# Routing without index transfers, six experts in whole float32 passes, SiLU taken from ScalarE's table

## The chip, the core and the metric

One core of one Trainium2 chip runs the whole program in one launch. The metric is device time in microseconds (us). The engines are PE (TensorE: matrix products; PEld is its weight load), DVE (VectorE), ACT (ScalarE), POOL (GpSimd) and SP (SyncE, which here only issues transfers). Each engine takes its own instructions strictly in the order in which they were written, and waits on semaphores for the others.

## What is computed

The reference, cut to what matters:

```python
# attention, 2 batches x 8 heads, 768 positions, 64 wide: a pair counts only if 6 sign bits of q@proj, k@proj agree
scores = where(q_bucket == k_bucket, q @ k.T / 8, -1e9)
x = (softmax(scores) @ v).reshape(1536, 512)          # 1536 tokens
# mixture of 8 experts, 192 tokens each, assigned greedily by descending logit
for idx in argsort(-(x @ w_gate).flatten()):
    tok, e = divmod(idx, 8)
    if assigned[tok] >= 0 or counts[e] >= 192: continue
    assigned[tok] = e; counts[e] += 1
for e in range(8): out[assigned == e] = relu(x[assigned == e] @ w1[e]) @ w2[e]   # 512 -> 1024 -> 512
# second layer on all tokens
h = out @ w_in; g = h / (1 + exp(-h)); result = g @ w_out                        # 512 -> 2048 -> 512
```

Everything is float32; `w_in` and `w_out` arrive as 64-bit floats and are turned into float32 on the chip.

## The kernel before, in words

**Attention** fills the first 280 us, and writes the tokens to a DRAM array `xd`. The change leaves its code alone.

**Routing** goes in eight phases (`route(ph)`). A phase fills one expert. It finds the logit at which some expert reaches 192 tokens by a search of seven counting steps (`count`): DVE compares all tokens with 63 to 78 thresholds (`cmp`, L577), PE sums the comparisons (L581, into `rp`), DVE turns the sums into a mask (`ok`, L584), PE picks the threshold (L587), DVE reads it (L588) and forms the next thresholds. So DVE and PE take turns, and the next phase needs the phase before. At the end stands the count of tokens per expert (`cnt`, L694). The next phase's head (L609 to L621: `pen`, `Lm`, `M`, `eq`, `mr`, `cthr`, `Bw`) needs only that count.

**Slots** (`slots(ph)`) turn a phase into a list of 192 tokens: the expert's number `ei` (L703 to L709, read by SP into a register, by which it loads that expert's weights), ranks (L713 to L719, a PE product `rpp` at L725, L729, L730), twelve one-hot matrices `oh` (L734), a product with the token numbers on PE (`rpi`, L740) and the integer list `TI` (L743). POOL then gathers the tokens from `xd` in two indirect transfers of 96 rows (L750, into `xg`), and PE transposes them (`px`, L757).

**An expert** (`expert(ph)`) is 8 blocks of a first product and 4 of a second. For the experts of phases 0 to FP-1 the product is in whole float32 (`whole`, L813; 4 matmuls of 192 columns are one planner's part). For the others the weights are split in a rounded half and a rest (`whi` on ACT, L781; `wlo` on POOL or DVE, L783), and the product is 4 matmuls of 384 columns (L800) and 4 of 192 (L801), whose halves ACT and DVE add (`t`, L789, L790), and split again (`H`, L842, `xhl`, L764).

**The second layer** (`second(gi)`) takes two experts' 384 tokens at once, in split form: A is 16 blocks of three products (L884); a block's sum `mm` goes through ACT (sigmoid, `sg`, L890), DVE (times `mm`, L891), ACT (rounded copy `gh`, L894) and DVE (rest `gl`, L895); B (L910) sums blocks into `acc`, which is scattered to the output by an indirect transfer (L919). The token list for that scatter is written by SP to a DRAM array `idxd` (L745) and read back as `ix` (L872). The weights of A and B are converted from 64-bit words once (`Weights.plan`): a load of half a megabyte into `craw` (L461), and passes on ACT (L465, for some halves L471) and DVE (L467, L468, L469, L470 or POOL L472), 28 halves in this part of the program.

**The order** on each engine comes from a planner (`Plan.run`, L38): every operation has a duration, a key and dependencies, and is taken by earliest start and then by key. Routing phases below `RU` have key -1e6, which lets nothing delay them by more than a tolerance; later ones come `RO` before their expert. `GA` is the planned transfer time of a gather, `dma` that of a weight load. These numbers steer only the order in which instructions are written; on the chip an instruction waits for its data, and all behind it on its engine wait too.

Of the kernel before, what the change touches and what calls it, by code (L numbers as in the profile page):

```python
# [9 lines left out]
F32 = mybir.dt.float32  # L10
# [414 lines left out]

FP = 4

NW = 4; NH = 3; NG = 4; NCW = 2

GROUPS = ((0, 1), (2, 3), (4, 5), (6, 7)); SKEW = (6, 0, 0, 0); RU = 2; RO = 250; CK = 200  # L430

GA = 3.4

# [7 lines left out]
class Weights:  # L441
# [10 lines left out]
    def plan(self, P, a, b, key, pool, ring, after=lambda m: []):  # L452

        nc=self.nc; V=nc.vector; raw={}
        for m in range(a,b):
# [17 lines left out]
            k=key+m  # L473
            P.op(("c64",m),"SP",.45,load,after(m),k,ring,dma=1.46)
            P.op(("cv",m,0),"Activation",.53,c0,[("c64",m)]+([("cv",m-1,0)] if h else []),k)
# [44 lines left out]

def moe(ctx, tc, L, xd, idxd, w1, w2, MW, K, ident, out):
    nc=tc.nc; V=nc.vector; G=nc.gpsimd; A_=nc.scalar
# [17 lines left out]
    Lc=c1.tile([128,12,8],F32,name="Lc")  # L540
    TI=c1.tile([96,16],I32,name="TI")
    def b12(x): return x[:,:,None].to_broadcast([128,12,8])
# [56 lines left out]
    def route(ph):  # L599
# [97 lines left out]
    def slots(ph):  # L697

        ch=Chain(("S",ph),[T_["end",ph]])
        def s0():  # L700
# [44 lines left out]
        def wr_(): nc.sync.dma_start(idxd[ph*192:(ph+1)*192,:].rearrange("(c p) o -> p (c o)",p=96),TI[:,2*ph:2*ph+2])  # L745
        op(("ix",ph),"SP",.2,wr_,[t],rk(ph),after=2.2)
        for c in range(2):
            def ga(c=c):
                xg=T_["xg",ph,c]=fx.tile([96,512],F32,name="xg",tag="xg")
                G.indirect_dma_start(out=xg,out_offset=None,in_=xd,in_offset=bass.IndirectOffsetOnAxis(ap=TI[:,2*ph+c:2*ph+c+1],axis=0))  # L750
            op(("g",ph,c),"Pool",1.25,ga,[t]+([("xt",ph-1,1)] if ph else []),rk(ph)+c*.01,dma=GA,slack=1.5)
# [115 lines left out]
    def second(gi):  # L867
        g=GROUPS[gi]; nt=3
        ydeps=[("Y",ph,db,1) for ph in g for db in range(4)]
        def ix():  # L870
            T_["IX",gi]=fx.tile([128,3],I32,name="ix",tag="ix")
            nc.sync.dma_start(T_["IX",gi],idxd[g[0]*192:g[0]*192+384,:].rearrange("(c p) o -> p (c o)",p=128))  # L872
        op(("IX",gi),"SP",.2,ix,[("ix",ph) for ph in g]+([("sc",gi-2,t) for t in range(3)] if gi>1 else []),0,after=2.2)
        for c in range(8):
            u=("A",gi,c); key=KEY[u]
            weights(u,2*c,([("cv",m,3) for m in (4*c,4*c+1) if m>=NC] if gi==0 else [("hi",("A",0,c))])+([("hi",("B",gi,c-2))] if c>1 else [("hi",("w2",g[-1],3))]+([("hi",("B",gi-1,7))] if gi else [])),key)
            for o in range(2):
# [14 lines left out]
                def gh(nm=nm):  # L892
# [40 lines left out]
def kernel(ctx: ExitStack, tc: tile.TileContext, q, k, v, proj, w_gate, w1, w2, w_in, w_out, out):  # L933
# [41 lines left out]
```

## Time and profile before

| | |
|---|---|
| median of 3 runs | 878.95 us (875.61 to 879.46) |
| profiled execution | 879.95 us, of which span 878.2 us |
| PE | 765.3 us busy, 87% of the span |
| DVE | 645.7 us busy, 74% |
| ACT | 446.5 us busy, 51% |
| POOL | 409.8 us busy, 47% |
| mean granted clock of TensorE | 0.916 |

Busy shares are averages over stages: attention to about 280 us, routing phase 0 alone to about 330 us, experts, routing and second layer mixed to about 704 us, and then PE without a pause to 870 us. What a change is worth is read from the stage in which it lies. The granted clock is 1.00 where the chip lets TensorE run at 2.4 GHz and 0.50 at 1.2 GHz.

### The profile page before, as it was taken

The page shows a single profiled execution, that of the slowest core. Times are in us where ns is not written, and L with a number is a line of the kernel's source. Part 1 is how long each engine was busy: PE and PEld are TensorE (multiplying, and loading weights), DVE is VectorE, ACT ScalarE, POOL GpSimd, SP SyncE. Part 2 cuts the span into 40 slices and gives each one's busy share as a digit, 9 for nine tenths or more (in the row PEclk, how much of TensorE's full clock was granted, in tenths as well). Part 3 has the DMA queues.
Part 4 walks back from the last instruction along what each step waited for, and adds up shares of the span by engine and source line. Part 5 has one row for each costly group of instructions (what it writes and reads, how often), then busy time and mean ns, then how long its engine had stood idle before and what let it go on. Part 6 is the DMA issues. An engine that isn't in the chain of part 4 may idle for free.

```text
span 878.2 us, 16341 instructions
## 1 busy us (share of the span) xinstructions
PE 765.3 (87%) x6117; PEld 675.4 (77%) x6117; DVE 645.7 (74%) x1541; ACT 446.5 (51%) x845; POOL 409.8 (47%) x295
## 2 busy tenths in 40 slices
PE   4988998999995349888998999897978999999996
PEld 3777887887784239776787888786868999999895
DVE  6788988869875887687899546798889576765441
ACT  2587887888884102153353232443443565655442
POOL 4276678778884000043443212244345554555442
PEclk9699999999997558896999799898998999999999
DMA  8958474763301265854364425401513732200000
GB/s 198 223 162 207 110 179 112 162 154 87 95 19 66 96 150 157 211 168 144 66 192 145 43 80 140 100 25 10 150 51 19 172 93 78 76 21 29 8 1 36
DMA packets 106559, 93.03 MB, mean 106 GB/s; under 512 B 33032, under 2 KB 92424, under 8 KB 106480
## 3 DMA queue, kind: packets, MB, share of 16 engines
q1 hardware_dynamic: 104496, 85.70, 36.8%
q0 software_dynamic: 1984, 6.29, 4.7%
q8 instruction: 48, 0.79, 0.4%
q14 instruction: 31, 0.25, 0.1%
HBM read 66.09 MB, written 6.30 MB: 82 GB/s over the span
## 4 chain that ended last, share of the span: by engine, by line
PE 55%; DVE 27%; issue 7%; DMA 5%; ACT 3%; POOL 2%; SPq 1%; POOLq 0%; DVEq 0%; ACTq 0%
PE mm L884 14%; PE acc L910 11%; PE mm L813 5%; PE mm L800 4%; PE S L300 3%; PE mm L801 3%; PE ST L340 2%; PE ST L341 2%; DMA xg<-xd,TI 2%; DVE wlo L783 2%; DVE cmp L577 2%; PE pm L232 2%; DVE S L302 2%; PE rp L581 2%; DVE m L304 2%
## 5 line engine op out<-in xcount | busy, mean ns | idle before, releaser
L350 POOL TENSOR_TENSOR AH<-Aa,AH 128x768 f16<-128x768 f32 x94 | 159.4, 1712 | 75.1 <-ACT AH L348 61.2
L783 POOL TENSOR_TENSOR wlo<-w,whi 128x512 fp32r<-128x512 f32 x68 | 106.0, 1563 | 138.3 <-ACT whi L781 115.2
L884 PE MATMUL mm<-Y,whi 128*128 128x384 f32 x512 | 113.2, 364 | 3.6 <-DVE ki L633 2.3
L884 PEld LDWEIGHTS mm<-Y,whi 128*128 128x128 f32 x512 | 94.7, 202 | 14.4 <-DVE sg L891 3.8
L345 ACT ACTIVATE Aa<-ST 128x384 f32<-128x384 f32 x192 | 87.8, 496 | 27.9 <-PE ST L341 26.9
L783 POOL TENSOR_TENSOR wlo<-wraw,whi 128x512 fp32r<-128x512 f32 x35 | 57.2, 1641 | 72.4 <-ACT whi L781 62.7
L300 PE MATMUL S<-k,q 76*128 76x384 f32 x192 | 74.1, 406 | 12.7 <-DVE m L304 5.8
L348 ACT CAST AH<-Aa 128x768 f16<-128x768 f32 x96 | 80.0, 835 | 0.8
L910 PE MATMUL acc<-whi,gh 128*128 128x512 f32 x192 | 79.9, 416 | 0.0
L581 PEld LDWEIGHTS <-cmp 128*63 128x63 bf16 (+2 forms) x588 | 33.1, 128 | 60.4 <-DVE cmp L577 45.2
L910 PE MATMUL acc<-wlo,gh 128*128 128x512 f32 x192 | 76.5, 398 | 0.0
L910 PE MATMUL acc<-whi,gl 128*128 128x512 f32 x192 | 76.3, 398 | 0.0
L781 ACT CAST whi<-w 128x1024 fp32r<-128x1024 f32 x64 | 67.0, 1047 | 16.9 <-PE acc L910 12.8
L340 PE MATMUL ST<-q,k 128*128 128x384 f32 x192 | 71.5, 372 | 1.4 <-ACT Aa L345 1.4
L783 DVE TENSOR_TENSOR wlo<-w,whi 128x512 fp32r<-128x512 f32 x60 | 53.3, 888 | 25.5 <-ACT whi L781 18.6
L341 PE MATMUL ST<-q,k 97*128 97x384 f32 x192 | 67.2, 350 | 0.7 <-ACT q L325 0.6
L581 PE MATMUL rp<-Bw,cmp 128*63 128x8 bf16 (+2 forms) x588 | 39.1, 185 | 32.2 <-DVE cmp L577 31.7
L364 PE MATMUL av<-vh,AH 128*128 128x66 f16 x576 | 63.6, 195 | 2.0 <-DVE AH L350 1.2
L362 PE MATMUL av<-vh,AH 128*128 128x66 f16 x576 | 64.5, 198 | 0.0
L302 DVE TENSOR_REDUCE S<-S 128x1 f32<-128x385 f32 x96 | 53.6, 559 | 14.6 <-PE S L300 13.7
L363 PE MATMUL av<-vl,AH 128*128 128x64 f16 x576 | 63.6, 194 | 0.0
L894 ACT CAST gh<-sg 128x384 fp32r<-128x384 f32 x64 | 32.7, 513 | 57.1 <-DVE sg L891 57.1
(253 smaller groups left out, 1955.5 us busy)
## 6 DMA issues: line engine op xcount, KB each, us to landing
wraw<-in_moe_w_dram SPq DMA_DIRECT2D x64, 512.0 KB
craw<-in_moe_w_in_dram SPq DMA_DIRECT2D x14, 512.0 KB
craw<-in_moe_w_out_dram SPq DMA_DIRECT2D x14, 512.0 KB
q<-qh SPq DMA_DIRECT2D x31, 192.0 KB
k<-kh SPq DMA_DIRECT2D x15, 384.0 KB
kn<-in_k_dram SPq DMA_DIRECT2D x16, 192.0 KB
qn<-in_q_dram SPq DMA_DIRECT2D x16, 192.0 KB
vn<-in_v_dram SPq DMA_DIRECT2D x8, 384.0 KB
```

Source lines behind the costliest of these rows:

```text
L300: nc.tensor.matmul(SX[y][:,:384],qq[:76,0,s],kk_[:76,0,s2],start=True,stop=True)
L302: if y==0: V.tensor_reduce(SX[0][:,mc0+c:mc0+c+1],SX[0][:,:385],axis=AX.X,op=ALU.max); return
L340: nc.tensor.matmul(ps[:,:384],kk_[:,1,s],qq[:,1,s2],start=True,stop=False)
L341: nc.tensor.matmul(ps[:,:384],kk_[:97,0,s],qq[:97,0,s2],start=False,stop=True)
L345: A_.activation(T_["A",g][:,m],T_["ST",u][:,:384],AF.Exp,scale=0.125)
L348: if e=="Activation": A_.copy(o[:,:,0],T_["A",g])
L350: def lo(e,g=g): (G if e=="Pool" else V).tensor_sub(T_["AH",g][:,:,1],T_["A",g],T_["AH",g][:,:,0])
L581: for b in range(6*h,6*h+6): nc.tensor.matmul(T_[k][:n,:8],cmp[h][:,b-6*h,:],T_["Bw",ph][:,b,:],start=b==0,stop=b==11)
L781: A_.copy(T_["w",u][0],get())
L783: s=slice(h*512,h*512+512); (G if e=="Pool" else V).tensor_sub(T_["w",u][1][:,s],get()[:,s],T_["w",u][0][:,s].bitcast(F32))
L884: nc.tensor.matmul(T_["ps",nm][:,:384],W(d,int(k==2)),T_["Y",gi][int(k==1)][:,d,:],start=k+d==0,stop=k==2 and d==3)
L910: nc.tensor.matmul(T_["acc",gi,t],a[:,s],x[:,o,:],start=c+o==0 and n==0,stop=c==7 and o==1 and n==2)
```

## The change

- The list of tokens goes no more through DRAM. `TI` becomes one tile of 128 x 4 for each group of two experts, laid out as the scatter wants it. The even expert of a group has its slots in rows of 128 and 64, the odd one of 64 and 128, and the odd one's first 64 are computed a second time at the partitions where the scatter reads them; so it has 36 products in place of 24, and three copies. Gathers are of 128 and 64 rows instead of 96 and 96.
- `FP` goes from 4 to 6: experts 4 and 5 use whole float32 passes.
- The second layer's activation is `Silu`, computed twice by ACT from `mm`: once as float32 and once rounded. DVE's multiplication is gone; the copy from `sg` becomes the second `Silu`.
- `RU` 2 to 4, `GA` 3.4 to 2.0, a conversion load's planned time 1.46 to 2.3, a head's 2.2 to 2.7, and some smaller ones. The slots of phase 0 come before everything, and the planner starts the conversion loads after the first gather.

```diff
-FP = 4
+FP = 6
-GROUPS = ((0, 1), (2, 3), (4, 5), (6, 7)); SKEW = (6, 0, 0, 0); RU = 2; RO = 250; CK = 200
-GA = 3.4
+GROUPS = ((0, 1), (2, 3), (4, 5), (6, 7)); SKEW = (6, 0, 0, 0); RU = 4; RO = 250; CK = 200
+GA = 2.0
-            op(nm,eng,dur,fn,self.last+list(deps),rk(self.name[1])+self.n*.001,ring,frees,after)
+            op(nm,eng,dur,fn,self.last+list(deps),rk(self.name[1])+self.n*.001-(1000 if self.name==("S",0) else 0),ring,frees,after)
+        gi,o_=divmod(ph,2); ti_=TI[gi]
+        parts=((3,0,64,0),(2,0,128,64)) if o_ else ((0,0,128,0),(1,0,64,128))
+        also=((1,64,128,0),) if o_ else ()
-            for c in range(2):
+            for c,r0,r1,f in parts+also:
                 for b in range(12):
-                    nc.tensor.matmul(p[:96,c:c+1],T_["oh",ph][:,b,c*96:(c+1)*96],tokid[:,b:b+1],start=b==0,stop=b==11)
+                    nc.tensor.matmul(p[r0:r1,c:c+1],T_["oh",ph][:,b,f:f+r1-r0],tokid[:,b:b+1],start=b==0,stop=b==11)
-        op(("ix",ph),"SP",.2,wr_,[t],rk(ph),after=2.2)
...
-                    T_["sg",nm]=fx.tile([128,384],F32,name="sg",tag="sg"); A_.activation(T_["sg",nm],src(),AF.Sigmoid)
-                def mu(nm=nm,src=src): s=T_["sg",nm]; V.tensor_tensor(s,s,src(),op=ALU.mult)
+                    T_["sg",nm]=fx.tile([128,384],F32,name="sg",tag="sg"); A_.activation(T_["sg",nm],src(),AF.Silu)
-                    A_.copy(T_["g",nm][0],T_["sg",nm])
+                    A_.activation(T_["g",nm][0],src(),AF.Silu)
...
-    MW.plan(P,NC,32,CK,cw,"craw")
+    MW.plan(P,NC,32,CK,cw,"craw",lambda m: [("g",0,1)])
```

**What it moves.** DVE, in routing phase 0, from the second counting step on. The rows `w` are a weight conversion. Before:

```order
L577 TENSOR_TENSOR cmp<-M,th 128x378 x2
L644 TENSOR_TENSOR shP<-sh_187,P 128x63
L467 TENSOR_SCALAR w_4939<-w_4939 128x512
L468 TENSOR_SCALAR w_4939<-w_4939 128x512
L584 TENSOR_TENSOR ok<-rp,cthr 63x8
L467 TENSOR_SCALAR w_4939<-w_4939 128x512
L468 TENSOR_SCALAR w_4939<-w_4939 128x512
L469 SCALAR_TENSOR_TENSOR w_4939<-craw,w_4939 128x512
L588 TENSOR_REDUCE C<-rp_4988 128x1
```

Now:

```order
L578 TENSOR_TENSOR cmp<-M,th 128x378 x2
L645 TENSOR_TENSOR shP<-sh_186,P 128x63
L585 TENSOR_TENSOR ok<-rp,cthr 63x8
L589 TENSOR_REDUCE C<-rp_4978 128x1
L652 TENSOR_TENSOR th<-shP,C 128x63
L654 TENSOR_TENSOR P<-P,C 128x1
```

No conversion stands in phase 0 any more; the first follows in phase 1, in its fourth counting step. In the same way SP issues no `craw` load before the first expert's four weight loads.

PE, around the end of routing phase 1 (`rpc`, the count) in the middle of expert 0. `mm<-xhl,wraw` is its first product, `mm<-H,wraw` its second. Before:

```order
L813 MATMUL mm<-xhl,wraw 128x192 x4
L690 LDWEIGHTS ones
L690 MATMUL rpc<-As,ones 128x8
L813 MATMUL mm<-xhl,wraw 128x192 x8
L725 LDWEIGHTS before
L725 MATMUL rpp<-tot,before 128x1
L813 MATMUL mm<-xhl,wraw 128x192 x4
L813 MATMUL mm<-H,wraw 128x192 x8
```

Now:

```order
L816 MATMUL mm<-H,wraw 128x192 x4
L691 LDWEIGHTS ones
L691 MATMUL rpc<-As,ones 128x8
L816 MATMUL mm<-H,wraw 128x192 x12
L726 LDWEIGHTS before
L726 MATMUL rpp<-tot,before 128x1
```

Before, 20 of expert 0's 64 matmuls stand ahead of that count; now 52 do. The first transposes (`px`) stood behind five of phase 1's counting steps; now they stand behind two.

DVE, from the expert's number of phase 1 on. `fm` opens the ranks of the slots, `pen` the head of phase 2. Before:

```order
L709 CAST ei<-ef 128x1
L713 TENSOR_TENSOR fm<-A_4903,newc 128x96
L715 TENSOR_REDUCE f<-fm 128x12
L717 SCALAR_TENSOR_TENSOR g_5578<-ones,f 128x12
L719 CAST tot<-g_5578 128x1
```

Now:

```order
L710 CAST ei<-ef 128x1
L610 TENSOR_SCALAR pen<-cnt 128x8
L612 TENSOR_TENSOR Lm<-Lc,pen 128x96
L613 TENSOR_REDUCE M<-Lm 128x12
L614 TENSOR_TENSOR eq<-Lm,M 128x96
```

The ten rows of the next phase's head now stand ahead of the ranks of phase 1, as they did in phase 0 before; for phase 0 itself they have moved behind the token list.

## Rows read from the trace of the kernel before

**Rows 1.** Busy time in five stages: us, PE, PEld, DVE, ACT, POOL, clock, DMA.

```profile
331.70:358.60 26.90, 26.17 (x183) 24.38 (x182) 19.81 (x73) 5.29 (x14) 3.57 (x2) 0.94 0.62 128
358.60:365.30 6.70, 3.90 (x41) 2.93 (x41) 5.73 (x22) 1.77 (x4) 0.00 (x0) 0.75 0.99 328
365.30:395.80 30.50, 26.43 (x175) 24.40 (x174) 23.26 (x48) 14.45 (x28) 9.92 (x7) 0.94 0.61 192
395.80:704.00 308.20, 283.44 (x1788) 247.42 (x1788) 237.24 (x624) 121.33 (x227) 115.60 (x85) 0.92 0.40 96
704.00:870.20 166.20, 165.75 (x896) 151.72 (x893) 96.67 (x154) 89.26 (x159) 81.35 (x49) 1.00 0.13 39
```

**Rows 2.** Timeline of PE, its long waits: start, us, ..., [idle before <-releaser].

```profile
406.81 0.16 PE L725 MATMUL rpp<-tot,before 128*128 128x1 bf16 x1 [2.77 <-DVE tot L719]
...
483.63 1.65 PE L884 MATMUL mm<-Y,whi 128*128 128x384 f32 x4 [2.34 <-DVE ki L633]
...
600.10 0.48 PE L581 MATMUL rp<-Bw,cmp 128*63 128x8 bf16 x6 [4.49 <-DVE cmp L577]
...
645.03 0.17 PE L587 MATMUL rp<-ok,ones 77*128 77x8 bf16 x1 [1.44 <-DVE ok L584]
```

**Rows 3.** Timeline of DVE in routing phase 0 and the start of phase 1.

```profile
292.46 1.02 DVE L577 TENSOR_TENSOR cmp<-M,th 128x378 bf16<-128x378 f32 x2
...
294.93 1.02 DVE L577 TENSOR_TENSOR cmp<-M,th 128x378 bf16<-128x378 f32 x2
...
300.78 1.20 DVE L577 TENSOR_TENSOR cmp<-k,thA 128x468 bf16<-128x468 f32 x2
...
309.12 0.16 DVE L609 TENSOR_SCALAR pen<-cnt 128x8 f32<-128x8 f32 x1
...
311.31 0.25 DVE L713 TENSOR_TENSOR fm<-A,newc 128x96 f32<-128x96 f32 x1
```

**Rows 4.** Timeline of POOL: the first gather.

```profile
318.73 1.15 POOL L750 DMA_INDIRECT xg<-xd,TI  x1 [45.38 <-DMA wraw<-in_moe_w_dram]
```

**Rows 5.** Timeline of PE: transposes of expert 0, first matmuls of experts 0 and 1.

```profile
329.55 1.38 PE L757 MATMUL px<-ident,xg 96*128 96x96 f32 x7 [1.60 <-DMA xg<-xd,TI]
...
331.67 2.91 PE L813 MATMUL mm<-xhl,wraw 128*128 128x192 f32 x8
...
365.29 2.93 PE L813 MATMUL mm<-xhl,wraw 128*128 128x192 f32 x8
```

**Rows 6.** Chain that ended last: expert 1's gather; parts of PE at full clock.

```profile
349.86 2.65 POOL xg L750
352.81 10.71 DMA xg<-xd,TI
...
419.40 1.04 PE rpi L740 x24
...
520.45 1.41 PE mm L813 x8
...
718.94 1.41 PE mm L800 x8
720.36 0.87 PE mm L801 x8
```

**Rows 7.** Instructions of one tile, `xg`: issue to landing of the 16 gathers.

```profile
DMA to landing us min/median/max: 7.0/7.9/11.6
```

**Rows 8.** Instructions of one line, L919: issue to landing of the 12 scatters.

```profile
DMA to landing us min/median/max: 2.7/3.5/5.9
```

**Rows 9.** Groups of instructions: line, engine, names, count | busy, mean ns | idle.

```profile
L891 DVE TENSOR_TENSOR sg<-sg,mm 128x384 f32<-128x384 f32 x64 | 35.1, 549 | 23.8 <-ACT sg L890 23.3
...
L783 POOL TENSOR_TENSOR wlo<-wraw,whi 128x512 fp32r<-128x512 f32 x35 | 57.2, 1641 | 72.4 <-ACT whi L781 62.7 <-DVE P L653 6.2 <-PE mm L884 3.4
...
L783 DVE TENSOR_TENSOR wlo<-wraw,whi 128x512 fp32r<-128x512 f32 x29 | 24.6, 850 | 15.8 <-ACT whi L781 15.2 <-PE mm L884 0.7
...
L842 DVE SCALAR_TENSOR_TENSOR H<-t,H 128x192 fp32r<-128x192 f32 x32 | 17.2, 558 | 1.0 <-ACT H L840 0.9
```

**Rows 10.** Timeline of DVE: one small instruction in two phases.

```profile
587.45 1.15 DVE L703 SCALAR_TENSOR_TENSOR newc<-cnt,closed 128x8 f32<-128x8 f32 x1
...
650.57 0.15 DVE L703 SCALAR_TENSOR_TENSOR newc<-cnt,closed 128x8 f32<-128x8 f32 x1
```

**Rows 11.** Timeline of POOL beside the first of these.

```profile
587.28 2.55 POOL L783 TENSOR_TENSOR wlo<-wraw,whi 128x512 fp32r<-128x512 f32 x2 [3.60 <-ACT whi L781]
```

More of the change, by code (lines that the diff above doesn't have):

```diff
@@ L473, in plan @@
             k=key+m
-            P.op(("c64",m),"SP",.45,load,after(m),k,ring,dma=1.46)
+            P.op(("c64",m),"SP",.45,load,after(m),k,ring,dma=2.3)
             P.op(("cv",m,0),"Activation",.53,c0,[("c64",m)]+([("cv",m-1,0)] if h else []),k)
@@ L519, in constants, with moe @@
     return j1i,ridx,thA,thB,w8,e8,slot,tokid,before,ones,unit,sh,th0
-def moe(ctx, tc, L, xd, idxd, w1, w2, MW, K, ident, out):
+def moe(ctx, tc, L, xd, w1, w2, MW, K, ident, out):
     nc=tc.nc; V=nc.vector; G=nc.gpsimd; A_=nc.scalar
@@ L540, in moe @@
     Lc=c1.tile([128,12,8],F32,name="Lc")
-    TI=c1.tile([96,16],I32,name="TI")
+    TI=[c1.tile([128,4],I32,name=f"TI{g}") for g in range(len(GROUPS))]
     def b12(x): return x[:,:,None].to_broadcast([128,12,8])
@@ L622, in route @@
         T_["Bw",ph]=None
-        ch("DVE",2.2 if ph else 1.6,head)
+        ch("DVE",2.7 if ph else 1.6,head)
         if not last:
@@ L709, in s0 @@
             V.tensor_copy(T_["ei",ph],ef)
-        a=ch("DVE",.8,s0)
+        a=ch("DVE",1.0,s0)
         def f0():
@@ L735, in slots, with ga @@
         for h in range(4): o=ch("DVE",.54,lambda h=h: oh(h))
+        gi,o_=divmod(ph,2); ti_=TI[gi]
+        parts=((3,0,64,0),(2,0,128,64)) if o_ else ((0,0,128,0),(1,0,64,128))
+        also=((1,64,128,0),) if o_ else ()
         def rows():
             p=T_["pi",ph]=psr.tile([128,512],F32,name="rpi",tag="rp")
-            for c in range(2):
+            for c,r0,r1,f in parts+also:
                 for b in range(12):
-                    nc.tensor.matmul(p[:96,c:c+1],T_["oh",ph][:,b,c*96:(c+1)*96],tokid[:,b:b+1],start=b==0,stop=b==11)
+                    nc.tensor.matmul(p[r0:r1,c:c+1],T_["oh",ph][:,b,f:f+r1-r0],tokid[:,b:b+1],start=b==0,stop=b==11)
         m=T_["m",ph]=ch("PE",1.1,rows,ring="rp")
         def ti():
-            V.tensor_copy(TI[:,2*ph:2*ph+2],T_["pi",ph][:96,:2])
-        t=ch("DVE",.1,ti,frees=[m])
-        def wr_(): nc.sync.dma_start(idxd[ph*192:(ph+1)*192,:].rearrange("(c p) o -> p (c o)",p=96),TI[:,2*ph:2*ph+2])
-        op(("ix",ph),"SP",.2,wr_,[t],rk(ph),after=2.2)
[L747 to L751, printed above, removed]
+            for c,r0,r1,f in parts+also: V.tensor_copy(ti_[r0:r1,c:c+1],T_["pi",ph][r0:r1,c:c+1])
+        t=T_["ti",ph]=ch("DVE",.2,ti,frees=[m])
+        for c,(col,r0,r1,f) in enumerate(parts):
+            def ga(c=c,col=col,r0=r0,r1=r1):
+                xg=T_["xg",ph,c]=fx.tile([128,512],F32,name="xg",tag="xg")
+                G.indirect_dma_start(out=xg[r0:r1],out_offset=None,in_=xd,in_offset=bass.IndirectOffsetOnAxis(ap=ti_[r0:r1,col:col+1],axis=0))
+            op(("g",ph,c),"Pool",1.25,ga,[t]+([("xt",ph-1,1)] if ph else []),rk(ph)+c*.01,dma=GA,slack=1.0)
         for h in range(2):
@@ L755, in xt @@
                 for d in range(2):
-                    for c in range(2):
-                        nc.tensor.transpose(ps[:,d*192+c*96:d*192+c*96+96],T_["xg",ph,c][:,(2*h+d)*128:(2*h+d+1)*128],ident[:96,:96])
+                    for c,(_,r0,r1,f) in enumerate(parts):
+                        nc.tensor.transpose(ps[:,d*192+f:d*192+f+r1-r0],T_["xg",ph,c][r0:r1,(2*h+d)*128:(2*h+d+1)*128],ident[r0:r1,r0:r1])
             def xh(h=h):
@@ L869, in second @@
         ydeps=[("Y",ph,db,1) for ph in g for db in range(4)]
[L870 to L873, printed above, removed]
         for c in range(8):
@@ L889, in sg, with gh @@
                 def sg(nm=nm,src=src):
-                    T_["sg",nm]=fx.tile([128,384],F32,name="sg",tag="sg"); A_.activation(T_["sg",nm],src(),AF.Sigmoid)
-                def mu(nm=nm,src=src): s=T_["sg",nm]; V.tensor_tensor(s,s,src(),op=ALU.mult)
-                def gh(nm=nm):
+                    T_["sg",nm]=fx.tile([128,384],F32,name="sg",tag="sg"); A_.activation(T_["sg",nm],src(),AF.Silu)
+                def gh(nm=nm,src=src):
                     T_["g",nm]=[fx.tile([128,384],F32R,name=x,tag=x,bufs=NG) for x in ("gh","gl")]
-                    A_.copy(T_["g",nm][0],T_["sg",nm])
+                    A_.activation(T_["g",nm][0],src(),AF.Silu)
                 def gl(nm=nm): x=T_["g",nm]; V.tensor_sub(x[1],T_["sg",nm],x[0].bitcast(F32))
                 op(("sg",nm),"Activation",.38,sg,sd,key,"sg")
-                op(("mu",nm),"DVE",.47,mu,[("sg",nm)],key,frees=fr)
-                op(("gh",nm),"Activation",.42,gh,[("mu",nm)],key)
+                op(("gh",nm),"Activation",.38,gh,[("sg",nm)],key,frees=fr)
                 op(("gl",nm),"DVE",.47,gl,[("gh",nm)],key,frees=[("sg",nm)])
@@ L917, in sc @@
             def sc(t=t):
-                ap=T_["IX",gi][:,t:t+1]
+                ap=TI[gi][:,t:t+1]
                 st=G.indirect_dma_start(out=out,out_offset=bass.IndirectOffsetOnAxis(ap=ap,axis=0),in_=T_["ot",gi,t],in_offset=None)
@@ L922, in second @@
             op(("ot",gi,t),"Activation",.48,ot,[("B",gi,15,t)],KEY["B",gi,7],"ot")
-            op(("sc",gi,t),"Pool",1.04,sc,[("ot",gi,t),("IX",gi)],KEY["B",gi,7],frees=[("ot",gi,t)],after=5.0)
+            op(("sc",gi,t),"Pool",1.04,sc,[("ot",gi,t)],KEY["B",gi,7],frees=[("ot",gi,t)],after=5.0)
     scat=[]
-    MW.plan(P,NC,32,CK,cw,"craw")
+    MW.plan(P,NC,32,CK,cw,"craw",lambda m: [("g",0,1)])
     for ph in range(8): route(ph); slots(ph)
@@ L939 @@
     xd = tc.dram_tile([1536, 512], F32, name="xd")
-    idxd = tc.dram_tile([1536, 1], I32, name="idxd")
     W = Weights(ctx, tc, w_in, w_out)
@@ L945 @@
     with ExitStack() as c2:
-        moe(c2, tc, L, xd, idxd, w1, w2, W, K[0], ident, out)
+        moe(c2, tc, L, xd, w1, w2, W, K[0], ident, out)
 _INS = ["q", "k", "v", "proj", "moe_w_gate", "moe_w1", "moe_w2", "moe2_w_in", "moe2_w_out"]
```

## The prediction

> **What bounds the kernel now.** I read first the busy shares by stage, then PE's long waits, then the routing on DVE, then the chain that ended last. The table by stage [rows 1] gives the frame. From 704 to 870.2 PE is busy 165.75 of 166.2 us at clock 1.00: nothing can be won there except by taking matmuls away, and the change leaves that code and its order alone. From 395.8 to 704 PE is busy 283.44 of 308.2 us, so 24.8 us are idle, and the mean clock is 0.92: part of the work runs at half speed after a wait. If the 8% of lost clock stretches the busy time by about as much, that is 12 to 25 us more; so waits cost 37 to 49 us in this stage, and I work with 45. PE's long waits there [rows 2] end on DVE: on `tot` at 406.81, `ki` at 483.63, `cmp` at 600.10, `ok` at 645.03, which are all routing. DVE is busy 237.24 of those 308.2 us: not the bound by its mean, but late in places. Before 331.7 the program is the routing of phase 0, DVE and PE in turns; the first gather [rows 4] is issued at 318.73 and the first product of expert 0 starts at 331.67 [rows 5], 12.9 us later.
>
> **The opening, won.** In phase 0 the conversions leave DVE. A clean counting step took 2.47 us there (292.46 to 294.93); the next one, with five conversion passes in it, 5.85 (294.93 to 300.78) [rows 3]. That is 3.4 us, less 0.9 of other work in that step; with the conversions that stand in later steps of the phase I take 5.7. Phase 1's head stood before the slots' ranks, from `pen` at 309.12 to `fm` at 311.31 [rows 3]: 2.2 us, which now stand behind the token list. With 0.4 for smaller waits the first gather is issued 8.3 us earlier, at 310.4. Expert 0 starts about 10 earlier, at 322: the 12.9 shrink by some 1.5, as no `craw` load is ahead of the weights in SP's order. At the least, if the gather is as slow as before, it is 7.
>
> **The opening, given back.** The order on PE now has 52 of expert 0's 64 matmuls ahead of phase 1's count, where 20 stood. Four cost 1.41 us at full clock [rows 6], so those 52 take 18.3 us. `px` stands ahead of all but two of phase 1's steps, so those wait on PE for the gather to land: 10.8 us from its issue to the transposes at 329.55 [rows 4, 5]. So the chain of phase 1 no longer runs while the gather flies. On DVE the conversions that left phase 0 now stand in phase 1 (four halves of four passes: some 8 us, at the 0.5 that each of the five passes cost in the step of 5.85), behind loads and ACT passes. I place phase 1's count at 347 instead of 340.7. Behind `ei` DVE then does phase 2's head (2.15 us, as from 309.12 to 311.31) before the ranks, and PE 36 products in place of 24 for the list: 24 took 1.04 [rows 6], so +0.5. The gather of expert 1 goes out at about 358 instead of 349.86, and takes with its issue 10.8 (13.7 before, with 10.71 of flight [rows 6]; it lay beside weight loads, with the DMA busy 0.99 in 358.6 to 365.3 [rows 1]). Expert 1's first product starts at about 371 instead of 365.29 [rows 5]: **+6**, between +3 and +10. PE then stands idle between the two experts for about 19 us, where it was 6.7 long [rows 1] before. The 8.3 us won are lost there, and more: the second gather, not the first, sets the time from here on.
>
> Expert 1's stretch takes as long as before (30.5 us [rows 1]), so A starts at 402 instead of 395.8. By then routing phase 2 and its slots are done as well, which stood later: 2.1 us of PE work leave the stage that follows. **-2.1**.
>
> **PE's work, added.** A part of a product costs 1.41 us in whole float32 (four matmuls of 192 columns). In halves it is 1.41 (four of 384) and 0.87 (four of 192) for two parts' worth [rows 6], 1.13 for one to compare. Experts 4 and 5 have 32 such parts: 32 x 0.28 = **+8.9**. This is on the path wherever PE is the bound. The 12 further products of phases 3, 5 and 7 cost 1.04 / 24 = 0.043 each: 36 x 0.043 = **+1.6**.
>
> **DVE and POOL, relieved.** DVE loses 64 multiplications, 35.1 us [rows 9]; half of L842, 8.6 of 17.2; as much again, about 8, of the sums beside it; 13 of its 29 `wlo`, 13 x 0.85 = 11; in all 63. About 54 of it lies between 395.8 and 704: three of four groups of multiplications (26) and all that belongs to experts 4 and 5. DVE's load there falls from 77% to 60%. POOL loses 19 of 35 `wlo`, 19 x 1.64 = 31 us. That also helps DVE: the same small instruction took 1.15 us while a `wlo` ran on POOL [rows 10, 11], and 0.15 when none did. Against this stand the conversions that the planner starts later: about 10 us of DVE in the stage of group 0, as much as the multiplications that leave it there. ACT has two passes for each `mm` as before, and is busy 121.33 of 308.2 [rows 1]: cover for a Silu that takes somewhat longer; without it, +0.1 us on 64 blocks would be 6. I take nothing.
>
> **What of the 45 goes.** The wait on `tot` at 406.81 goes, since `rpp` of phase 2 now comes with work ahead of it: about 10 with the slow clock behind it. The waits of phases 4 to 6 are on DVE behind `wlo`, multiplications and POOL's contention. Each costs, with the slow clock behind it, more than its own idle time: I estimate 9 us lost around 480, 8 around 600 and 9 from 641 to 677, and take away two thirds, 17. New waits come: 4 for late conversions behind group 0, 2 for gathers. That makes -23 (-10, -17, +6, and -2 for the smaller ones). The ends are 0 (freed time lies where nobody waits) and -37 (all but the new ones and a rest of 8). No row shows the stage with this DVE load; I sit nearer the middle because half of the stage's waits keep their cause, the turns of DVE and PE in a search of 35 to 40 us. **-23**, so 22 are left.
>
> **The sum.** +6 - 2.1 + 8.9 + 1.6 - 23 = -8.6. Against the profiled execution (878.2 of span and 1.75 around it, 879.95) that is 871.4; the median of the runs is 1.0 below that profile. I say 871. Without the relief of waits the change would cost 14.4; it breaks even when 31 of the 45 remain.
>
> **Rivals.** *Slower: the gap between experts 0 and 1.* PE is idle there about 19 us and its clock falls with it, and the freed DVE time doesn't lie where PE waits. For: the order on PE, 52 matmuls before the count, is certain; and of the 63 us not one lies in the search of a phase. Against: the waits of rows 2 are behind DVE work that goes. If 40 of the 45 are left, 871 + 18 = 889, about 888; it decides from 33 on. *No change*: the stalls shrink by the 14 that the added work costs, 880.
>
> *The gather lands quickly.* Its landing took 7.0 us at the least and 7.9 in the median [rows 7], but the scatters, indirect too and with rows of the same 2 KB, had 2.7 and 3.5 [rows 8]. If the gathers were slow because conversion and weight loads stood in the queues beside them, which the later `craw` loads now spare the first ones, then `px` holds phase 1 up by 4 to 5 less, and expert 1's gather is as much shorter: 8 off, 863. Against: even the quickest of 16 gathers took 7.0.
>
> The Trainium skill (DMA: Bandwidth & Descriptors, section "Anatomy of one DMA — SWDGE (gpsimd) path") gives such a transfer about 2.0 us plus its bytes over 436 GB/s. That would be an estimate of 2.6 us for 128 rows of 2 KB, and by it this rival would be the rule. This trace disagrees, with 7.0 at the least, so its chance stays small.
>
> *The activation is not the one function twice.* If ACT had to load another table whenever it goes from the experts' Relu to Silu, that would lie in the path of every `mm`. The changed program holds two table loads in all, as many as before, so I give it no chance of its own.
>
> **How the numbers follow.** My forecast has 0.60, with its own range 860 to 878; slower by the gap 0.20 (888); no change 0.10 (880); quick gathers 0.10 (863). What a measurement of this kernel can tell from no change is about 0.5%, 4.4 us. Faster than 874.6: most of the forecast (0.47) and the quick gathers (0.08), 0.55. Slower than 883.3: the gap rival and a tail of the others, 0.23. The same: 0.22. The range 857 to 888 reaches from expert 1 eight earlier and a few more stalls gone to the slower rival.
>
> **What would show it.** The opening: first gather near 310, first product of expert 0 near 322, phase 1's `rpc` near 347, expert 1's first product near 371, A's first near 402. If A's first is below 397, the given-back part was too dear. The added work: 768 matmuls at the whole-float32 line, and 8 to 9 us more for experts 4 and 5. The relief: PE's idle time between A's start and the last routing falls from 24.8 to about 12, with the clock nearer 0.96, and no wait behind `tot` of phase 2. The tail: still about 166 us from the last wait, at clock 1.00. I am wrong in the main step if PE's idle time there stays above 18, and wrong in the opening if PE isn't idle for over 12 us between experts 0 and 1.

## The result: 856.2 us against 879.2, and the profile after

The changed kernel takes 856.23 us (median of 4 runs, 854.11 to 859.19) against 879.21 for the kernel before; the ratio is 0.973 (95% interval 0.967 to 0.980). The forecast was 871, with a range of 857 to 888: the direction is right, the gain was nearly three times what I said, and the time lies just under the range. The profiled execution has a span of 854.8 us, 23.4 less than before.

First the changed kernel by stage: us, then busy time (and instructions) of PE, PEld, DVE, ACT and POOL, the granted clock, the DMA share and GB/s. The stages are first gather to first product, expert 0, the gap, expert 1, the mixture from A's first product on, and the tail.

```profile
312.20:323.60 11.40, 6.02 (x48) 4.07 (x48) 6.38 (x26) 1.51 (x3) 2.44 (x2) 0.50 0.64 219
323.60:352.00 28.40, 27.03 (x195) 24.78 (x195) 22.38 (x77) 7.10 (x17) 0.00 (x0) 0.94 0.57 170
352.00:369.20 17.20, 9.51 (x93) 6.87 (x91) 13.61 (x54) 2.08 (x4) 1.95 (x2) 0.56 0.55 172
369.20:403.60 34.40, 29.86 (x201) 27.32 (x200) 26.05 (x79) 8.94 (x19) 7.57 (x6) 0.87 0.48 153
403.60:680.00 276.40, 271.68 (x1779) 235.22 (x1778) 187.56 (x524) 102.86 (x199) 95.18 (x67) 0.99 0.36 113
680.00:846.00 166.00, 165.64 (x901) 153.24 (x900) 90.69 (x123) 86.61 (x158) 80.59 (x49) 1.00 0.13 39
```

Against [rows 1], A begins 7.8 us later (403.6 for 395.8), the stage behind it is 31.8 shorter (276.4 for 308.2), and the tail is as long as it was. So the whole gain, and more, lies in one stage. PE's idle time there fell from 24.8 to 4.7 us and its clock rose from 0.92 to 0.99. As a measure for all that follows I take what PE loses in that stage: its length less PE's busy time at the granted clock. Before it is 308.2 - 283.44 x 0.92 = 47.4 us, now 276.4 - 271.68 x 0.99 = 7.4. (The clock has two digits, so each is good to about 1.4 us.) The long waits of [rows 2] are gone. PE's four largest sums of waits in that stage before (engine, line, waited for, us in total, times, longest):

```profile
PE rp L581 <- DVE cmp L577: 11.0, 9, 4.5
PE rp L587 <- DVE ok L584: 6.3, 4, 2.9
PE rpp L725 <- DVE tot L719: 4.4, 2, 2.8
PE mm L884 <- DVE ki L633: 2.3, 1, 2.3
```

Now these are all that PE has left from A's start to the tail:

```profile
PE mm L816 <- DVE Y L866: 3.6, 1, 3.6
PE rpp L726 <- DVE tot L720: 0.7, 1, 0.7
PE rp L582 <- DVE cmp L578: 0.4, 1, 0.4
```

The opening, on DVE: clean counting steps in phase 0 (the one that took 5.85 us with conversions in it [rows 3] takes 3.28), and the head of phase 1 behind the token list.

```profile
293.02 1.02 DVE L578 TENSOR_TENSOR cmp<-M,th 128x378 bf16<-128x378 f32 x2
295.49 1.02 DVE L578 TENSOR_TENSOR cmp<-M,th 128x378 bf16<-128x378 f32 x2
298.77 1.20 DVE L578 TENSOR_TENSOR cmp<-k,thA 128x468 bf16<-128x468 f32 x2
...
306.21 0.25 DVE L714 TENSOR_TENSOR fm<-A,newc 128x96 f32<-128x96 f32 x1
...
311.12 0.22 DVE L748 CAST TI<-rpi 128x1 int32<-128x1 f32 x2 [1.01 <-PE rpi L745]
311.26 0.15 DVE L610 TENSOR_SCALAR pen<-cnt 128x8 f32<-128x8 f32 x1
```

POOL's first gathers of experts 0 and 1, for [rows 4]:

```profile
312.24 1.16 POOL L753 DMA_INDIRECT xg<-xd,TI  x1 [36.04 <-DVE M L613]
...
356.63 0.91 POOL L753 DMA_INDIRECT xg<-xd,TI  x1 [41.64 <-DVE TI L748]
357.84 1.04 POOL L753 DMA_INDIRECT xg<-xd,TI  x1 [0.30 <-issue]
```

PE, for [rows 5]: the transposes and first products of experts 0 and 1, phase 1's count between them, phase 2's `rpp` and A's start.

```profile
319.01 0.48 PE L760 MATMUL px<-ident,xg 128*128 128x128 f32 x1 [0.36 <-DMA xg<-xd,TI]
...
323.58 2.93 PE L816 MATMUL mm<-xhl,wraw 128*128 128x192 f32 x8
...
345.65 0.17 PE L691 MATMUL rpc<-As,ones 128*128 128x8 bf16 x1
...
363.78 0.95 PE L582 MATMUL rp<-Bw,cmp 128*63 128x8 bf16 x12 [1.42 <-DVE cmp L578]
364.66 2.87 PE L760 MATMUL px<-ident,xg 64*128 64x64 f32 x8
...
369.17 2.93 PE L816 MATMUL mm<-xhl,wraw 128*128 128x192 f32 x8
...
397.08 0.16 PE L726 MATMUL rpp<-tot,before 128*128 128x1 bf16 x1 [3.57 <-DVE tot L720]
...
403.62 1.66 PE L883 MATMUL mm<-Y,whi 128*128 128x384 f32 x8
```

The gathers land in half the time: the line of [rows 7] (7.0/7.9/11.6 before) now reads

```profile
DMA to landing us min/median/max: 3.1/4.0/6.7
```

The groups that answer to [rows 9]: the multiplication is gone, 16 `wlo` of the experts are left on each engine, 16 of L842's (now L845).

```profile
L786 POOL TENSOR_TENSOR wlo<-wraw,whi 128x512 fp32r<-128x512 f32 x16 | 28.2, 1762 | 37.2 <-ACT whi L784 36.2 <-PE mm L883 1.0
...
L786 DVE TENSOR_TENSOR wlo<-wraw,whi 128x512 fp32r<-128x512 f32 x16 | 11.1, 693 | 18.1 <-ACT whi L784 17.4 <-PE mm L883 0.7
...
L845 DVE SCALAR_TENSOR_TENSOR H<-t,H 128x192 fp32r<-128x192 f32 x16 | 9.6, 625 | 0.5 <-ACT H L843 0.5
```

One group grew that the prediction has no term for: PE's transposes of the gathered tokens, 64 in blocks of 96 rows before, 32 of 128 and 32 of 64 now. Before, now, and in the run b_gather (below), which has the kernel before's work with the new blocks:

```profile
L757 PE MATMUL px<-ident,xg 96*128 96x96 f32 x64 | 9.6, 297 | 2.4 <-DMA xg<-xd,TI 2.4
L760 PE MATMUL px<-ident,xg 128*128 128x128 f32 (+1 forms) x64 | 17.1, 327 | 0.9 <-DMA xg<-xd,TI 0.9
L757 PE MATMUL px<-ident,xg 128*128 128x128 f32 x64 | 18.1, 340 | 5.1 <-DMA xg<-xd,TI 5.1
```

Behind A's start alone they went from 5.97 to 11.29 us. In the stage, PE's busy time at the granted clock rose by 8.2 us (283.44 x 0.92 to 271.68 x 0.99).

### The profile page after: what moved, and what is told of

Read it like the earlier page. It is cut to its first block, busy times and chain, and to the rows that moved or that the text cites. A ratio compares the mean times of both kernels' runs of the same rounds, so it can differ in the third digit from the quotient of the medians.

```text
span 854.8 us, 16202 instructions
## 1 busy us (share of the span) xinstructions
PE 765.5 (90%) x6165; PEld 671.2 (79%) x6165; DVE 586.4 (69%) x1432; ACT 418.6 (49%) x805; POOL 385.4 (45%) x276
## 4 chain that ended last, share of the span: by engine, by line
PE 72%; DVE 19%; issue 4%; ACT 2%; DMA 1%; POOL 1%; POOLq 0%; SPq 0%; DVEq 0%; ACTq 0%
PE mm L883 16%; PE acc L907 14%; PE mm L816 13%; PE S L300 4%; PE rp L582 3%; PE ST L340 3%; PE mm L803 3%; PE ST L341 2%; PE pm L232 2%; PE px L760 2%; DVE S L302 2%; PE mm L804 2%; PE av L362 2%; DVE m L304 1%; PE av L364 1%
## 5 line engine op out<-in xcount | busy, mean ns | idle before, releaser
L883 PE MATMUL mm<-Y,whi 128*128 128x384 f32 x512 | 104.1, 344 | 0.4 <-ACT gh L892 0.4
L883 PEld LDWEIGHTS mm<-Y,whi 128*128 128x128 f32 x512 | 88.2, 188 | 2.0 <-ACT gh L892 0.5
L300 PE MATMUL S<-k,q 76*128 76x384 f32 x192 | 74.9, 411 | 12.8 <-DVE m L304 5.9
L893 DVE TENSOR_TENSOR gl<-sg,gh 128x384 fp32r<-128x384 f32 x64 | 56.9, 891 | 34.0 <-ACT gh L892 33.9
L816 PE MATMUL mm<-H,wraw 128*128 128x192 f32 x384 | 73.6, 344 | 3.6 <-DVE Y L866 3.6
L786 DVE TENSOR_TENSOR wlo<-w,whi 128x512 fp32r<-128x512 f32 x60 | 50.5, 843 | 36.6 <-ACT whi L784 26.7
L816 PE MATMUL mm<-xhl,wraw 128*128 128x192 f32 x384 | 74.6, 346 | 0.0
L889 ACT ACTIVATE sg<-mm 128x384 f32<-128x384 f32 x64 | 31.6, 493 | 81.9 <-PE mm L883 74.5
L816 PEld LDWEIGHTS mm<-H,wraw 128*128 128x128 f32 x384 | 66.2, 199 | 6.0 <-DVE Y L866 3.7
L753 POOL DMA_INDIRECT xg<-xd,TI x16 | 18.2, 1138 | 107.5 <-DVE TI L748 63.6
L816 PEld LDWEIGHTS mm<-xhl,wraw 128*128 128x128 f32 x384 | 65.3, 199 | 0.6
```

What stands on the lines that cost most here:

```text
L300: nc.tensor.matmul(SX[y][:,:384],qq[:76,0,s],kk_[:76,0,s2],start=True,stop=True)
L786: s=slice(h*512,h*512+512); (G if e=="Pool" else V).tensor_sub(T_["w",u][1][:,s],get()[:,s],T_["w",u][0][:,s].bitcast(F32))
L816: for i in range(k,k+4): nc.tensor.matmul(T_["ps",nm][:,:192],w(i),xs(i),start=i==0,stop=i==n-1)
L883: nc.tensor.matmul(T_["ps",nm][:,:384],W(d,int(k==2)),T_["Y",gi][int(k==1)][:,d,:],start=k+d==0,stop=k==2 and d==3)
```

## Experiments

Theory W: the waits went because DVE and POOL lost work. Theory P: they went because the planner's new numbers write an order that fits the chip. Each ratio is to the kernel before on the same chip. The stage runs from A's first product to 174.6 us before the end of the span, which leaves the tail out. In the tail PE loses another 5 us in a_dve, 4 in b_fp6_silu and 3.5 in b_fp5, and at most 1.4 in every other run. Names that begin with a or o start from the changed kernel (o with the planner's old numbers), with b from the kernel before. The planner orders every kernel anew, so a run changes not only the work that it names but also the order of the instructions; no run here holds the order still while DVE's load changes.

| run | median us | ratio (95%) | stage from A's start | DVE busy in it | PE loses in it |
|---|---|---|---|---|---|
| before | 879.2 | | 308.2 | 237.2 | 47.4 |
| changed | 856.2 | 0.973 (0.967 to 0.980) | 276.4 | 187.6 | 7.4 |
| a_fp4 | 874.4 | 0.992 (0.989 to 0.996) | 295.4 | 223.8 | 32.6 |
| a_mult | 864.6 | 0.980 (0.976 to 0.985) | 280.0 | 201.3 | 9.5 |
| a_oldplan | 857.0 | 0.972 (0.966 to 0.979) | 287.3 | 183.6 | 14.5 |
| b_newplan | 906.8 | 1.022 (1.013 to 1.031) | 315.7 | 239.9 | 56.5 |
| b_gather | 889.5 | 1.009 (1.006 to 1.013) | 314.3 | 239.6 | 47.4 |
| b_fp6 | 858.2 | 0.973 (0.970 to 0.977) | 283.3 | 196.2 | 18.5 |
| b_silu | 862.9 | 0.978 (0.973 to 0.982) | 287.7 | 220.7 | 29.4 |
| a_ru2 | 872.9 | 0.991 (0.987 to 0.994) | 297.4 | 202.0 | 24.8 |
| a_fp8 | 859.7 | 0.978 (0.972 to 0.984) | 280.5 | 184.7 | 7.4 |
| b_fp6_silu | 853.2 | 0.970 (0.964 to 0.975) | 276.6 | 190.0 | 7.3 |
| a_ixwrite | 897.8 | 1.019 (1.013 to 1.026) | 306.8 | 187.2 | 43.0 |
| o_ru3 | 852.0 | 0.968 (0.963 to 0.974) | 279.1 | 185.6 | 10.0 |
| b_fp5 | 869.6 | 0.989 (0.984 to 0.994) | 299.3 | 212.4 | 32.8 |
| a_dve | 867.2 | 0.987 (0.982 to 0.992) | 287.1 | 211.7 | 13.1 |
| a_pool | 862.8 | 0.982 (0.977 to 0.987) | 282.1 | 203.3 | 14.0 |
| o_ru3_late | 853.5 | 0.971 (0.964 to 0.977) | 281.8 | 201.1 | 12.1 |

### One relief undone in the changed kernel: a_fp4, a_mult

```diff
-FP = 6
+FP = 4
```

> The changed kernel with FP back at 4: experts 4 and 5 in rounded halves, all else as changed. Theory W (the waits went because DVE and POOL lost work): about 28 us of DVE and 31 us of POOL work come back into the stage from A's start on, and waits with them, so the 9 us of matmuls saved are lost again: 862 to 872 us. Theory P (the waits went because the planner's new numbers and dependencies write an order that fits the chip): the waits stay away and PE saves its 9 us: 846 to 850 us.

874.4 us: W, and 2 us above its range. Of the 25 us that PE loses again 14 are idle time (4.7 to 18.8 us) and the rest is the lower clock, 0.95 for 0.99. They come back on DVE, as the first two of the three largest waits of this kernel in the stage show; the third stood there before (columns as above):

```profile
PE mm L883 <- DVE t L793: 7.7, 2, 4.4
PE rp L582 <- DVE cmp L578: 6.3, 3, 5.5
PE mm L816 <- DVE Y L866: 3.6, 1, 3.6
```

The other relief undone (b_silu, below, is the reverse of this on the kernel before):

```diff
-A_.activation(T_["sg",nm],src(),AF.Silu)
+A_.activation(T_["sg",nm],src(),AF.Sigmoid)
+V.tensor_tensor(s,s,src(),op=ALU.mult)
-A_.activation(T_["g",nm][0],src(),AF.Silu)
+A_.copy(T_["g",nm][0],T_["sg",nm])
```

> The changed kernel with the activation as before: sigmoid on ACT, multiplication on DVE, copy on ACT. Theory W: 35 us of DVE work come back, 26 of them in the stage with the waits: 862 to 872 us. Theory P: the multiplications stand beside other work, 855 to 860 us.

864.6, on W's side; but its profiled execution (span 857.5) is a good one among its runs, so the 9.5 of the table are low for it. With experts 4 and 5 relieved, the multiplication costs less than it won by itself.

### Numbers without work, work without numbers: a_oldplan, b_newplan, a_ru2

```diff
-RU = 4; GA = 2.0; dma=2.3; head 2.7; s0 1.0; slots of phase 0 -1000; gathers slack=1.0; craw after ("g",0,1)
+RU = 2; GA = 3.4; dma=1.46; head 2.2; s0 .8; (none); slack=1.5; (none)
```

> The changed kernel's work with all planner numbers of before (RU 2, GA 3.4, conversion load 1.46, head 2.2, s0 0.8, slack 1.5, no priority of phase 0's slots, conversion loads not after the first gather). Theory W: the relief stays, only the opening is lost: 856 to 863 us. Theory P: the waits come back: 870 to 880 us.

> The kernel before with only the planner's numbers and dependencies of the changed one. Theory W: DVE is as loaded as before, so the waits stay: 875 to 885 us. Theory P: most of the waits go: 858 to 868 us.

857.0 and 906.8. P is refuted from both sides as the reason of the gain: the old numbers keep it, and the new ones alone make the kernel before 2.2% slower. W missed the second as well (875 to 885), for it left out that an order can also cost. In b_newplan the slow gathers (median landing 11.4 us) meet an order written for quick ones, and PE waits 12.0 us on `px` in the stage where the kernel before had no such wait. RU alone put back:

> The changed kernel with RU back at 2, so that phases 2 and 3 have no precedence. Theory W: 854 to 860 us. Theory P, if RU is the number that matters: phases 2 and 3 come late again and PE waits on their DVE work, 865 to 875 us.

872.9, as P says for RU; but since the old numbers as a set cost nothing, it is a mixed set of numbers that costs here, not RU 2. PE waits for `cmp`, `tot` and `oh` of late phases again, and it loses 24.8 us with DVE busy for 202, where a_mult loses 9.5 with DVE busy for 201. So the loss does not follow from DVE's load alone; the order can add some 15 us to it.

### One relief alone on the kernel before: b_fp6, b_silu, both, and half a dose

```diff
-FP = 4
+FP = 6
```

> The kernel before with FP 6 alone: 9 us more matmuls, 28 us less on DVE, 31 less on POOL. Theory W: the waits of phases 4 to 6 shrink by 10 to 20 us, 868 to 878 us. Theory P: the matmuls are added and the waits stay, 884 to 890 us.

> The kernel before with Silu twice on ACT and no multiplication on DVE. Theory W: 26 us less DVE in the stage with the waits, 862 to 872 us. Theory P: 876 to 881 us.

858.2 and 862.9 us, better than W had it for the first. Each relief alone wins most of what the whole change won. The stage in both (columns as in the table by stage), first FP 6:

```profile
398.70:682.00 283.30, 275.85 (x1786) 241.81 (x1786) 196.20 (x566) 99.02 (x187) 89.24 (x66) 0.96 0.45 102
```

Silu alone:

```profile
401.50:689.20 287.70, 271.90 (x1788) 239.51 (x1788) 220.65 (x596) 118.58 (x226) 111.56 (x79) 0.95 0.43 103
```

> The kernel before with FP 6 and Silu, that is the changed one without the new token list and with the planner's old numbers. Alone they gave 858 and 863 us. If both reliefs take away the same waits (theory W with overlap), together 850 to 857 us; if they add, 840 us. Against the run with the planner's old numbers and the new token list (857) it prices the token list by itself: 0 if gathers were not on the path, 4 to 8 us slower if they were. Gather landing 7 us or more if the index writes are what delays it.

853.2 us: they don't add, since PE loses 47.4, 18.5 or 29.4, and 7.3 with both (11 with the tail); a rest stays. Nor is this kernel slower than the changed one: without the new token list and the new numbers the gain is the same. With FP 5:

> The kernel before with FP 5: half of the relief of FP 6 (14 us of DVE, 15 of POOL) for half of the added matmuls. FP 6 gave -23. If waits go in proportion to the relief: 868 to 871 us. If they go once DVE has a little slack in the place where PE waits: 858 to 865. If expert 5's passes are what counts: 876 to 881.

869.6, as proportion has it: half the relief, 1.1% of the 2.7% that FP 6 gave. No threshold shows at this one point between; the waits shrink with the load.

### Which engine's relief: a_dve, a_pool

```diff
 if not split:
+    if u[1] in (4,5):   # the same with nc.gpsimd and range(1)
+        x=wh.tile([128,1024],F32R,name="wlo",tag="wlo")
+        for h in range(2): nc.vector.tensor_sub(x[...],r[...],r[...])
```

> The changed kernel with 32 further DVE subtractions of 128 x 512 beside the loads of experts 4 and 5 (27 us of DVE, into a scratch tile, used by nobody). If DVE's load in that stretch is what made PE wait, 863 to 872 us, as with FP 4; if not, 856 to 859.

> The changed kernel with 16 further POOL subtractions of 128 x 512 beside the loads of experts 4 and 5 (26 us of POOL, into a scratch tile, used by nobody). If POOL's passes slow DVE's small instructions enough to matter, 860 to 866 us; if POOL's relief is worth nothing by itself, 855 to 859.

867.2 and 862.8. The scratch tile is taken from the buffers of `wlo`, but what grew is PE's waits on DVE: one of 3.5 us on `t` in the tail of a_dve, and those on `tot` from 0.7 to 3.8 us in a_pool. Both engines count: by the ratios 27 us of DVE cost 1.4%, 12 us, and 26 us of POOL 0.9%, 7 us. Together that is about what FP 4 put back (18 us, with some 5 us of matmuls saved). DVE's busy time in the stage is 16 us higher in a_pool than in the changed kernel, with the same number of DVE instructions (524 there); this agrees with the slowing beside POOL that [rows 10, 11] showed on one instruction:

```profile
405.73:687.80 282.07, 273.57 (x1782) 237.09 (x1780) 203.30 (x525) 102.84 (x200) 115.44 (x83) 0.98 0.35 109
```

### What the matmuls cost: a_fp8

> The changed kernel with FP 8: experts 6 and 7 in whole float32 as well. In the changed kernel the waits in the stage of the mixture are down to about 7 us, so there is nothing left for this relief to win. If a whole part costs 0.28 us more than a pair of halves, as the chain's rows say, the 32 parts add 9 us: 863 to 867 us. If it costs less than that, because the smaller experts 4 and 5 already added only 4 to 6, it comes to 859 to 862. If DVE and POOL still hold PE up, 850 to 856.

859.7; its span is 4.5 us over the changed kernel's, of which 0.6 lies ahead of A. So 32 whole parts cost about 4, not 9. The chain of waits shows a part of the reason, late in the program with the clock at 1.00. Changed kernel, two parts in halves, 1.41 and 0.87, as in [rows 6]:

```profile
709.00 1.41 PE mm L803 x8
710.41 0.87 PE mm L804 x8
```

Here, one part in whole float32:

```profile
705.69 1.30 PE mm L816 x8
```

1.30, where I had taken 1.41 from [rows 6]: 32 x (1.30 - 1.14) = 5.1. In the chain of the kernel before such a part takes 1.30 to 1.50 us at full clock, so one row could not price it.

### Why the gathers are quick: b_gather, a_ixwrite

```diff
-for c in range(2): (96 rows)
+for c,(n,f) in enumerate(((128,0),(64,128))): (products, TI copies, gathers, transposes; idxd written in two pieces)
```

> The kernel before with its gathers of 128 and 64 rows instead of 96 and 96 (and the index array written in two pieces); order and work otherwise as before. If the shape of the gather sets its landing, the median goes from 7.9 us to 3.5 to 4.5, and expert 0 and 1 start 3 to 4 us earlier each: 870 to 877 us. If the landing hangs on the weight and conversion loads beside it, it stays at 7 to 8 us and the time at 877 to 881.

889.5, above both ranges: the shape doesn't make the gathers quick. They landed later than before, median 10.8 us, in a kernel that now writes the list in two pieces. And the shape has a price of its own: PE loses as much in the stage as in the kernel before, but its transposes there take 12.24 us for 5.97, and the stage is 6 us longer. The reverse, on the changed kernel:

```diff
+for col,r0,r1,f in parts: nc.sync.dma_start(idxd[ph*192+f:ph*192+f+r1-r0,:],ti_[r0:r1,col:col+1])
```

> The changed kernel, which also writes each list of tokens to DRAM as the kernel before did (192 elements of 4 bytes, read by nobody). If these writes are what delayed the gathers, the median landing goes from 4.0 to between 7 and 11 us and px waits for it, 858 to 866 us. If not, 3 to 4.5 us and 855 to 858.

897.8 us, far beyond what I expected of it, from 768 bytes for each expert that nobody reads. The landings:

```profile
DMA to landing us min/median/max: 6.5/10.9/15.8
```

The gathers' and scatters' queue takes over twice the time for the same packets. Changed kernel (packets, MB, share of 16 engines):

```profile
q0 software_dynamic: 1984, 6.29, 2.2%
```

With the writes:

```profile
q0 software_dynamic: 1984, 6.29, 5.1%
```

and PE waits on what came at once before; the two longest of its waits from 320 us to the tail:

```profile
PE rp L582 <- DVE cmp L578: 19.5, 10, 9.8
PE px L763 <- DMA xg<-xd,TI: 17.7, 10, 6.4
```

So the index writes delay the gathers: this run adds no other work. How much of the 41 us is the landing, and how much SP, which now waits for each list with weight loads queued behind it, was not told apart.

### A better version? o_ru3, o_ru3_late, and a comparison on one chip

```diff
-RU = 2   (a_oldplan)
+RU = 3   (o_ru3; o_ru3_late also loads craw after the first gather)
```

> The changed kernel's work with the planner's old numbers, but RU 3: phase 2 of the routing has precedence too. With the old numbers A began 10 us earlier than in the changed kernel and 10 us of waits were left behind it. If phase 2 coming earlier takes those away and A keeps its start, 846 to 852 us; if the opening then pays for it, 855 to 860.

> The changed kernel's work with the planner's old numbers, RU 3, and the conversion loads after the first gather. With RU 3 and the old numbers it was 852. The first gather comes 6 to 8 us earlier. If expert 1 keeps its place behind expert 0, A starts 3 to 6 earlier and the run takes 846 to 850 us; if the conversions then hold up the second gather, as in the changed kernel, 851 to 857.

852.0 and 853.5. The earlier first gather is worth nothing in either order. Side by side in five rounds:

> The changed kernel as it is, once more, beside the next run on the same chip. 854 to 858 us, ratio to the kernel before 0.970 to 0.976.

> The changed kernel's work with the planner's old numbers and RU 3, beside the changed kernel on the same chip. If the new numbers' later start of A costs what the earlier profiles show (A at 399.4 against 403.6, 2.5 of it lost in the stage behind), 850 to 855 us, 0.2% to 0.6% under the changed kernel; if they cost nothing, the same within 0.2%.

The changed kernel gave 857.66 (0.973, 0.969 to 0.976), o_ru3 854.67 (0.971, 0.967 to 0.975). The runs of the two overlap, so no difference is shown; no version of these is better than the changed kernel beyond its uncertainty.

## Why the prediction was wrong, step by step

**The opening, right.** First gather 312.2 (forecast 310.4), expert 0 at 323.6 (322), phase 1's count at 345.7 (347), second gather at 356.6 (358), expert 1 at 369.2 (371), A at 403.6 (402). The gap with its slow clock is there: 17.2 us at 0.56. By the letter of its last sign the prediction would still be wrong here: it wanted PE idle for over 12 us between the experts, and PE is idle for 7.7, since phase 2's counting, expert 1's list and its transposes fill the other 9.5. The step of 5.85 us [rows 3] held six conversion passes and not five, which priced them at 0.5 instead of 0.42 us each; that is about 1 us. One detail failed: phase 2's wait on `tot` didn't go, it moved ahead of A (3.57 us at 397.08), and expert 1's stretch, with that wait and the clock at 0.87 behind it, took 34.4 us where I had 30.5.

**PE's added work, right by luck.** +8.9 was forecast for experts 4 and 5; a_fp8 measures 4 to 5 for as many parts. +1.6 was forecast for the products of the token list; they took 12.9 us before and 12.8 now. The transposes were not in the sum: the change cuts 192 tokens into 128 and 64 instead of 96 and 96, which I gave no term, and it cost 7.5 us (17.1 for 9.6), 5.3 of them behind A's start. The errors cancel: -2.1 + 8.9 + 1.6 = 8.4 was forecast for the stage, 8.2 measured.

**What of the 45 goes: the step that failed.** The size of the loss was right (45, measured 47.4). I took 23 off it, place by place: 10 for the wait on `tot`, "two thirds" of 26 at three places, 2 for smaller ones, and 6 back for new waits; half of the waits, I wrote, "keep their cause, the turns of DVE and PE in a search". The loss fell by 40. The searches of phases 3 to 6 lie behind A's start in both kernels, and yet PE's waits on `cmp` and `ok` there fell from 17.3 to 0.4 us: the turns are not a fixed price, and what PE waited for was mostly the other work that DVE did between them. Of the 6 us of new waits one of 3.6 came, on `Y`. DVE's relief there was sized nearly right (54 forecast, 237.2 - 187.6 = 49.6 measured). What failed is the exchange: 0.43 us of loss per us of relief in my sum, 40 / 49.6 = 0.8 in the run. Each relief alone, from the loaded kernel, stands above 0.43 as well: 18 for the 16.6 us of DVE that the multiplications took (b_silu, 1.1), 29 for 41 with POOL's relief in it (b_fp6, 0.7), 12 for 25 with the tail counted (b_fp5, 0.5). Load put back into the relieved kernel cost less: in a_dve 24 us on DVE made the stage 10.7 longer (0.44). With 4.5 in place of 8.9, nothing for the products, 5.3 for the transposes, -40 in place of -23 and A's start at +7.8 the sum is 7.8 - 2.1 + 4.5 + 5.3 - 40 = -24.5; the span fell by 23.4, and the difference is within the rounding of the clock.

**The relief's two halves.** My sum was right in counting DVE and POOL, but it never asked what FP 6 or Silu alone would give. That would have shown that they overlap: against the kernel before on the same chip b_fp6 won 23 us, b_silu 18.5, and both 26.

**The rivals.** *The gap* came as forecast, but decided nothing, as the loss behind it fell to 7. *Quick gathers* came true as a landing (4.0 us), for another reason than the one I gave: not the conversion loads (a_oldplan has them early again, and 3.3 us) but the index writes. It didn't give its 8 us: expert 0's `px` waited only 0.36 and 0.53 us for its gathers, but 52 matmuls of expert 0 stood ahead of phase 1's count anyway, and expert 1's `px` at 364.66 stood behind counting steps of phase 2. The rule of the Trainium skill that I had set aside (DMA: Bandwidth & Descriptors, section "Anatomy of one DMA — SWDGE (gpsimd) path"; an estimate of 2.6 us for 128 rows) now stands nearer: the trace has 3.1 at the least. Most of what lay above that in the kernel before came with the index writes, as a_ixwrite shows (median 4.0 without and 10.9 with them).

**Token list and planner's numbers.** I held the opening against the relief and added them. In fact the old list and numbers with both reliefs run at 853.2: these two edits together are worth nothing that can be measured. The new list brings quick gathers and dearer transposes, and without the new numbers it neither wins nor loses (a_oldplan, 857.0); the new numbers lose much without the new list (b_newplan) or with the index writes put back (a_ixwrite).

## What to carry to other kernels

Where PE's waits in a stage all end on one helper engine, take the stage's whole loss (length less busy time at the granted clock) as what can be won, and not a share per place: here each us of relief took 0.5 to 1.1 us of it away while much was left. Then ask what each edit would win alone, since reliefs of one loss don't add. An order written for quick transfers won nothing measurable here with them, and cost 2.2% in the kernel whose transfers were slow. Take the price of an added operation from several of its rows, not from one, and give a term to every operation whose shape the change alters.

## What the runs showed of the hardware that I had not expected

192 indices of 4 bytes, written to DRAM at the time of a gather of 192 rows of 2 KB, held the gathers up by some 7 us: the median landing was 4.0 us without and 10.9 with them (in two pieces), on separate queues. In the eight kernels with such writes beside their gathers (the kernel before, b_newplan, b_gather, b_fp5, b_fp6, b_silu, b_fp6_silu, a_ixwrite) the median lay between 7.9 and 11.4, in the ten without them between 3.3 and 4.6.

The Trainium skill (DMA: Bandwidth & Descriptors, section "Specifications") says that below 512 B the DMA engine does a read-modify-write. That fits with the cost of these writes in its direction; no run here shows the mechanism.

The same 1536 tokens cost PE 9.6 us in 64 float32 transposes of 96 rows, and 17.1 us in 32 of 128 and 32 of 64 (18.1 in b_gather). No run shows why.
